# Attention and two gated feed-forward layers in one kernel: the decay rows of k move to ScalarE's queue, and the order of the first loads changes

## The chip, the core and the metric

The kernel runs on one core of a Trainium2 chip. The metric is the time of one execution on the device in microseconds. Three runs of the kernel before took 955.3, 936.14 and 935.29 us; their median is 936.14.

TensorE (PE) multiplies matrices, VectorE (DVE) and ScalarE (ACT) do elementwise work and reductions, GpSimd (POOL) does some of the elementwise work. DMAs are issued from two queues here: SyncE's (SP), which does nothing else, and ScalarE's, where an issue stands between the computing instructions and is reached only when those ahead of it have been handed on.

## The reference

Four batches with eight heads, 576 positions and head size 64 go through attention with a forget gate; the eight heads of a token are then joined to 512 columns, and 2304 tokens go through two feed-forward layers, all of it in float32 by the reference:

```python
scores = scale * np.matmul(q, k.transpose(0, 1, 3, 2))
log_f = np.log(np.clip(f, 0.0001, 1.0))
cum = np.cumsum(log_f, axis=-1)
decay = cum[:, :, :, None] - cum[:, :, None, :]
scores = np.where(causal, -1000000000.0, scores + decay)
attn = softmax(scores)                      # over the last axis
x = np.matmul(attn, v)                      # heads joined: 2304 x 512
h = x @ w_in;  g = h * np.tanh(softplus(h));  x = g @ w_out      # 512 -> 2048 -> 512
out = (sigmoid(x @ w_gate) * (x @ w_val)) @ w_out2               # 512 -> 1536 -> 512
```

The weights arrive as 64-bit floats, read as pairs of 32-bit words.

## The kernel before, in words

**Tiling.** Batch by batch, heads are taken in pairs (four pairs a batch). For each pair the scores of 128 queries against all earlier keys go into PSUM, VectorE adds the causal mask and takes the maximum (`softmax_part`, line 713), ScalarE takes the exponential with the sum (line 764 in the first batch's first part, 862 elsewhere), the weights of attention are transposed and multiplied with v (lines 967 and 979). In the first batch scores are float32 matmuls of 66 rows: 64 of the head, and two that add the decay. One operand, `Q32` (tile `sab`), holds q in rows 0 to 63, the running sum of log f in row 64, and a constant in row 65. The other, `K32` (tile `mab`), holds k in rows 0 to 63, a constant in row 64, and the running sum in row 65. The product of these two rows is the decay.

**The decay rows.** `decay()` loads f, clips it, takes the logarithm, and forms the running sum with one scan on VectorE (line 463) into a float32 tile `cum` (in the trace and the order a piece of `wout`, `wout_90`). Four small DMAs (line 469) copy it into the rows: for q and for k one each for the first 144 positions (`seg` 0) and the next 112 (`seg` 1). The first score of a pair needs only the first piece of k's row, the second (256 columns wide) both. The constants come from memory: line 405 for k's tile, line 407 for q's.

**The other loads at the start.** `prep_first` loads k (line 550) and q (line 552) of a pair, `prep_v` its v (line 623), `constants` an identity matrix (line 397), and `load_w` half a group of weights, 512 KB (line 669). The first four weights, numbers 0 to 3, go out on ScalarE's queue; VectorE turns their 64-bit words into float32 in three passes (lines 641, 645, 649), then ScalarE forms a 16-bit high part (line 506) and VectorE, GpSimd or ScalarE with GpSimd the low part (lines 525, 530 and 534).

**What sets the order.** Every piece of work is a generator that asks for an engine with an estimated duration; `Order` runs a small planner at build time. Each piece has a due time (the second argument of `spawn`, or `od.due`), and of the pieces that could start on an engine the one with the earliest due time goes first. The plan becomes each engine's fixed list of instructions. A load on SP also waits in the plan until the planner's DMA clock is near. The planner decides, too, which engine does a copy or a low part (`scaled`, `rest`), and where it expects TensorE to wait it inserts filler matmuls on the mask (`fill`, line 1085) that compute nothing of use. A change of a due time at the start therefore shifts decisions through the whole program.

**Completion semaphores.** All DMAs, from both queues, take one of eight completion semaphores in turn (DMAHW0 to DMAHW7 in the order). A DMA is issued only once the one that had the same semaphore eight DMAs earlier has landed; that wait stands on the issuing queue and holds everything behind it.

Of the kernel before, what the change touches and what calls it, by code (L numbers as in the profile page):

```python
# [58 lines left out]
class Order:  # L59
# [32 lines left out]
    def spawn(self, gen, due):  # L92
        self.n += 1
        t = {"time": self.now(), "due": due, "n": self.n, "gen": gen, "lag": 0.0}
        self.step(t, None)
# [214 lines left out]
def attention_moe_moe_kernel(ctx, tc, qk, v, f, carry, ident, const, rows_q, rows_k, w_in, w_out, w_gate, w_val, w_out2, out):  # L310
    nc = tc.nc
# [29 lines left out]
    od = Order(BUFS)  # L341
    done, give, pick, spawn = od.done, od.give, od.pick, od.spawn

    def take(*tags, turn=()):
        return (yield ("take", tags, *turn))

    def need(*keys):
        yield ("need", keys)
# [22 lines left out]
    def words(t, o, n):  # L371
        return t.rearrange("p a b c -> p (a b c)")[:, o:o + n]
# [18 lines left out]
    KF = 66  # L391
    K32 = MAB.rearrange("p a q h s -> p a q (h s)").bitcast(FP32)
    Q32 = SAB.rearrange("p a q h s -> p a q (h s)").bitcast(FP32)
# [41 lines left out]
    def decay():  # L435
# [26 lines left out]
        yield "DVE", t_dve(SL)  # L462
        nc.vector.tensor_tensor_scan(out=cum, data0=ft, data1=zt, initial=car, op0=ALU.add, op1=ALU.add)

        for row, key in ((Q32[64:65], "rq"), (K32[65:KF], "rk")):
            for seg in range(2):
                n = min(SL, 256 - seg * SL)
                yield "SP", 0.5, 10000, (key, seg)
                nc.sync.dma_start(
                    out=row.rearrange("o a q s -> o (a q) s")[:, :, seg * SL:seg * SL + n],  # L470
                    in_=cum[seg * NH:seg * NH + 2 * NPB, 0:n],
                )
# [180 lines left out]
    def load_w(hi, lo, src, scale, key, n):  # L653

        if n:
            yield from need(("st", n - 1) if n < NFIRST else ("rk", 1))

        if n in XPLACE:
            yield from take(turn=("wr", n))
            raw = words(XPLACE[n], 0, 2048)  # L660
        else:
            (ri,) = yield from take("wr", turn=("wr", n))
            raw = words(xt[2 + (ri % 3 == 0)], ri % 3 // 2 * 2048, 2048)
        raw = raw.bitcast(I32).rearrange("p (n t) -> p n t", t=2)
        due = od.cur["due"]
        if n < NFIRST:
            od.due((-40, -30.1, -28.8, -27.8)[n])
        yield "SP", 0.5, 128 * 4096
        (nc.scalar if n < NFIRST else nc.sync).dma_start(
            out=raw.rearrange("p n t -> p (n t)").rearrange("p (a n) -> p a n", a=src.shape[1]), in_=src  # L670
        )
        od.due(due)
        (fi,) = yield from take("wf", turn=("wf", n))
        w = words(xt[4], fi % 2 * 1024, 1024).bitcast(I32)
        yield from float32(w, raw)
        if n not in XPLACE:
            give("wr", ri)
        w = w.bitcast(FP32)
        if len(hi.shape) == 3:
            w = w.rearrange("p (a n) -> p a n", a=hi.shape[1])  # L680
        yield from scaled(hi, w, scale, 512)
        yield from rest(lo, w, scale, hi, 512, WP0 <= n < WPOOL)
        give("wf", fi)
        done(key)
# [856 lines left out]
    NFIRST = 4  # L1541
    XPLACE = {2: win[5], 3: win[4]}
    spawn(decay(), -50)
    nl = ns = no = 0
    for b in range(NB):

        if b:
            end = ((b * S + 256) // 256) * 8 - LEAD
            mid = end - SPAN
            beg = mid - SPANA  # L1550
            if b == 1:
                beg, mid = beg + LATE, mid + LATE
            spans = ((beg, mid), (mid, end))
        else:
            end = at_step[1, 0] - LEAD
            mid = end - B0
            beg = -30.0
            spans = ((beg, beg + 4.5), (mid, end), (end + 1, end + 1 + C4))
        pre = PRE if b else 0.0
        for p in range(NPB):  # L1560
            spawn(prep(b, p, 0, ("ld", nl)) if b else prep_first(p, 0, ("ld", nl)), beg + p - pre)
            nl += 1
            if b == 0 and p == 3:
                spawn(constants(), beg)
                spawn(masks(), beg)
                spawn(ones(), beg - 1)
# [97 lines left out]
```

## Time and profile before

| what | value |
|---|---|
| runs | 955.3, 936.14, 935.29 us |
| profiled execution, its own time | 933.85 us |
| its span, first to last instruction | 932.1 us |
| mean granted clock of TensorE | 0.989 |
| busy: PE, DVE, ACT, POOL | 907.0, 591.5, 556.9, 74.9 us |
| DMA traffic | 90.50 MB, mean 97 GB/s |

The profiled execution takes 1.75 us more than its span, and it is 2.3 us under the median of the runs. Busy time is a mean over stages with different limits: TensorE is busy 97% of the span, yet that share holds fillers and the slow first stage. A row of a timeline gives the start in us from the span's start, the duration, engine, line, operation and tiles, the number of instructions merged into it, and in square brackets how long the engine had been idle before and what released it. ACTq and SPq are the queues that issue DMAs: the duration there is that of the issue, not of the transfer. A transfer's landing has no row of its own; it shows as the release of whoever waited for it.

### The profile page before, as it was taken

The numbers are of one execution on the slowest core, as the hardware profiler recorded it, in microseconds if no ns is written. First come the engines' busy times: TensorE is split into PE (matmuls) and PEld (weight loads), VectorE is DVE, ScalarE is ACT, GpSimd is POOL, SyncE is SP. The second block draws the span as 40 slices with busy tenths as digits, with TensorE's granted clock in tenths as the row PEclk, the third lists the DMA queues.
The fourth block names the chain that finished last, engine by engine and source line by source line (L and its number), as shares of the span: only waits on it lengthen the run. The fifth ranks groups of instructions, "written<-read, shape, count | busy, mean of one in ns | idle before, by whom it ended". The sixth has DMA issues, their size and how long they took to land.

```text
span 932.1 us, 20975 instructions
## 1 busy us (share of the span) xinstructions
PE 907.0 (97%) x8599; PEld 715.8 (77%) x8599; DVE 591.5 (63%) x1352; ACT 556.9 (60%) x1093; POOL 74.9 (8%) x75
## 2 busy tenths in 40 slices
PE   7999899999999999999999999999999999999998
PEld 5667678778887888878888887777777777777776
DVE  5889989766667745675799999963236133432333
ACT  4878689788888977978445465544325332432343
POOL 0011211111111101000100010110000000000000
PEclk7989999999999999999999999999999999999999
DMA  6687986568457655644344433200000000100000
GB/s 203 185 189 191 228 241 169 119 122 160 120 124 136 122 135 107 119 91 71 105 136 136 148 129 109 69 12 34 1 1 35 13 1 1 47 1 2 12 36 23
DMA packets 145426, 90.50 MB, mean 97 GB/s; under 512 B 103626, under 2 KB 127138, under 8 KB 145329
## 3 DMA queue, kind: packets, MB, share of 16 engines
q1 hardware_dynamic: 144242, 87.07, 38.3%
q10 hardware_dynamic: 1088, 2.10, 0.7%
q8 instruction: 67, 1.10, 0.5%
q14 instruction: 29, 0.23, 0.1%
HBM read 50.79 MB, written 4.84 MB: 60 GB/s over the span
## 4 chain that ended last, share of the span: by engine, by line
PE 66%; DVE 10%; DMA 4%; ACT 2%; issue 1%; SPq 0%; ACTq 0%; DVEq 0%
PE bank L1358 8%; PE bank L1360 8%; PE bank L1359 8%; PE o_acc L1506 5%; PE o_acc L1505 5%; PE o_acc L1504 5%; PE h_ps L1070 4%; PE y_ps L1120 4%; PE h_ps L1072 4%; PE h_ps L1071 4%; PE y_ps L1122 4%; PE y_ps L1121 4%; PE o_ps L979 3%; DMA wraw<-w_gate 2%; DVE wf L649 2%; DVE wf L645 1%
## 5 line engine op out<-in xcount | busy, mean ns | idle before, releaser
L1120 PE MATMUL y_ps<-g,wout 128*128 128x256 f16 x576 | 157.2, 273 | 2.8 <-ACT wout L506 2.2
L1121 PE MATMUL y_ps<-g,wout 128*128 128x256 f16 x576 | 157.0, 273 | 2.4 <-DVE wout L525 2.4
L1070 PE MATMUL h_ps<-xt,win 128*128 128x256 f16 x576 | 157.3, 273 | 2.0 <-ACT h_ps L1033 1.2
L1071 PE MATMUL h_ps<-xt,win 128*128 128x256 f16 x576 | 156.9, 272 | 0.1
L1122 PE MATMUL y_ps<-g,wout 128*128 128x256 f16 x576 | 157.0, 273 | 0.0
L1072 PE MATMUL h_ps<-xt,win 128*128 128x256 f16 x576 | 156.9, 272 | 0.0
L1448 DVE TENSOR_TENSOR v<-bank,e 128x512 f32<-128x512 f32 (+1 forms) x30 | 19.1, 637 | 165.2 <-ACT bank L1365 164.9
L1365 ACT ACTIVATE bank<-bank 128x512 f32<-128x512 f32 (+1 forms) x90 | 48.5, 539 | 92.8 <-PE bank L1360 90.7
L525 DVE SCALAR_TENSOR_TENSOR pp<-sp,sm,pp 128x512 f16<-128x512 f32 (+4 forms) x126 | 80.5, 653 | 20.1 <-ACT pp L506 19.0
L713 DVE CUSTOM_DVE_ANT_0 sp<-s_ps,mask 128x512 f32<-128x512 f32 (+4 forms) x144 | 67.2, 492 | 17.6 <-PE s_ps L847 14.8
L862 ACT ACTIVATE sp<-sp,sm 128x384 f32<-128x384 f32 (+3 forms) x112 | 63.7, 570 | 15.8 <-DVE sm L713 15.2
L506 ACT ACTIVATE pp<-sp,sm 128x384 f16<-128x384 f32 (+4 forms) x112 | 65.1, 603 | 7.3 <-DVE sm L738 3.5
L1070 PEld LDWEIGHTS <-win 128*128 128x128 f16 x576 | 56.2, 98 | 17.0 <-issue 3.4
L1071 PEld LDWEIGHTS <-win 128*128 128x128 f16 x576 | 56.4, 98 | 11.3 <-issue 2.6
L1120 PEld LDWEIGHTS <-wout 128*128 128x128 f16 x576 | 56.3, 98 | 11.2 <-ACT wout L506 2.7
L1121 PEld LDWEIGHTS <-wout 128*128 128x128 f16 x576 | 56.3, 98 | 10.7 <-DVE wout L525 3.0
L1043 DVE SCALAR_TENSOR_TENSOR g<-h_ps,g 128x512 f16<-128x512 f32 x72 | 49.3, 687 | 23.1 <-ACT g L1039 22.9
L1072 PEld LDWEIGHTS <-win 128*128 128x128 f16 x576 | 56.2, 98 | 7.0 <-issue 0.3
L1122 PEld LDWEIGHTS <-wout 128*128 128x128 f16 x576 | 56.3, 98 | 6.5
L1033 ACT ACTIVATE h_ps<-h_ps 128x512 f32<-128x512 f32 x72 | 41.8, 584 | 14.0 <-PE h_ps L1072 13.7
L979 PEld LDWEIGHTS <-vt 128*64 128x64 f16 x1368 | 36.2, 112 | 14.2 <-issue 12.9
L534 POOL TENSOR_TENSOR low<-st,mab 128x512 f16<-128x512 f32 (+1 forms) x24 | 32.4, 1352 | 160.8 <-ACT mab L506 144.7
(208 smaller groups left out, 2290.4 us busy)
## 6 DMA issues: line engine op xcount, KB each, us to landing
xt<-w_out SPq DMA_DIRECT2D x16, 512.0 KB
xt<-w_in SPq DMA_DIRECT2D x12, 512.0 KB
wraw<-w_gate SPq DMA_DIRECT2D x12, 512.0 KB
wraw<-w_val SPq DMA_DIRECT2D x12, 512.0 KB
wraw<-w_out SPq DMA_DIRECT2D x12, 512.0 KB
out<-ob SPq DMA_DIRECT2D x18, 256.0 KB
vst<-v SPq DMA_DIRECT2D x12, 320.0 KB
st<-qk SPq DMA_DIRECT2D x12, 320.0 KB
```

Source lines behind the costliest of these rows:

```text
L506: nc.scalar.activation(out=dst, in_=src, func=ACTF.Copy, scale=scale, bias=bias)
L525: nc.vector.scalar_tensor_tensor(dst, a, scale, b, op0=ALU.mult, op1=ALU.subtract)
L713: nc.vector.tensor_tensor_reduce(out=sp, in0=ps_ap, in1=mk, op0=ALU.add, op1=ALU.min, scale=-0.125, scalar=1.0e38, accum_out=mn,)
L1070: nc.tensor.matmul(dst, lhsT=wh, rhs=xh, start=(k == 0), stop=False)
L1071: nc.tensor.matmul(dst, lhsT=wh, rhs=xl, start=False, stop=False)
L1072: nc.tensor.matmul(dst, lhsT=wl, rhs=xh, start=False, stop=(k == KD - 1))
L1120: nc.tensor.matmul(dst, lhsT=wh, rhs=gh, start=first, stop=False, skip_group_check=True)
L1121: nc.tensor.matmul(dst, lhsT=wl, rhs=gh, start=False, stop=False, skip_group_check=True)
L1122: nc.tensor.matmul(dst, lhsT=wh, rhs=gl, start=False, stop=last, skip_group_check=True)
L1358: nc.tensor.matmul(dst, lhsT=wh, rhs=xh[:, k], start=first, stop=False, skip_group_check=True)
L1359: nc.tensor.matmul(dst, lhsT=wh, rhs=xl[:, k], start=False, stop=False, skip_group_check=True)
L1360: nc.tensor.matmul(dst, lhsT=wl, rhs=xh[:, k], start=False, stop=last, skip_group_check=True)
```

## The change

Four edits. The rows of k (`rk`) are issued by ScalarE instead of SP, and the two loops are turned round, so that the order is q and k of piece 0, then q and k of piece 1. The third and fourth weights are issued by SP instead of ScalarE, and the first two weights get earlier due times. The second weight is no longer held in the plan until the third and fourth wait for the rows. The first two pairs of q and k get due times ahead of the rows.

```diff
--- before.py
+++ after.py
@@ -462,11 +462,11 @@
         yield "DVE", t_dve(SL)
         nc.vector.tensor_tensor_scan(out=cum, data0=ft, data1=zt, initial=car, op0=ALU.add, op1=ALU.add)
 
-        for row, key in ((Q32[64:65], "rq"), (K32[65:KF], "rk")):
-            for seg in range(2):
+        for seg in range(2):
+            for row, key in ((Q32[64:65], "rq"), (K32[65:KF], "rk")):
                 n = min(SL, 256 - seg * SL)
                 yield "SP", 0.5, 10000, (key, seg)
-                nc.sync.dma_start(
+                (nc.scalar if key == "rk" else nc.sync).dma_start(
                     out=row.rearrange("o a q s -> o (a q) s")[:, :, seg * SL:seg * SL + n],
                     in_=cum[seg * NH:seg * NH + 2 * NPB, 0:n],
                 )
@@ -653,7 +653,7 @@
     def load_w(hi, lo, src, scale, key, n):
 
         if n:
-            yield from need(("st", n - 1) if n < NFIRST else ("rk", 1))
+            yield from need(("st", 0) if n == 1 else ("rk", 1))
 
         if n in XPLACE:
             yield from take(turn=("wr", n))
@@ -664,9 +664,9 @@
         raw = raw.bitcast(I32).rearrange("p (n t) -> p n t", t=2)
         due = od.cur["due"]
         if n < NFIRST:
-            od.due((-40, -30.1, -28.8, -27.8)[n])
+            od.due((-49.95, -49.5, -28.8, -27.8)[n])
         yield "SP", 0.5, 128 * 4096
-        (nc.scalar if n < NFIRST else nc.sync).dma_start(
+        (nc.scalar if n < 2 else nc.sync).dma_start(
             out=raw.rearrange("p n t -> p (n t)").rearrange("p (a n) -> p a n", a=src.shape[1]), in_=src
         )
         od.due(due)
@@ -1558,7 +1558,9 @@
             spans = ((beg, beg + 4.5), (mid, end), (end + 1, end + 1 + C4))
         pre = PRE if b else 0.0
         for p in range(NPB):
-            spawn(prep(b, p, 0, ("ld", nl)) if b else prep_first(p, 0, ("ld", nl)), beg + p - pre)
+
+            ahead = 19.9 + 0.9 * p if b == 0 and p < 2 else 0
+            spawn(prep(b, p, 0, ("ld", nl)) if b else prep_first(p, 0, ("ld", nl)), beg + p - pre - ahead)
             nl += 1
             if b == 0 and p == 3:
                 spawn(constants(), beg)
```

In the program that comes of it the lists of all engines differ. Two places matter at the start, and VectorE's list shows what they do to it.

SP from its fourth row on (after the loads of f and of the matrix that carries the sums), before; `mab` is k's tile, `sab` q's, `wout_90` the running sums, `win_83` the identity, `xt_72` v:

```order
L405 DMA mab<-const 1x4608
L407 DMA sab<-const 1x2560
L550 DMA mab<-qk 64x2x256
L552 DMA sab<-qk 64x2x256
L397 DMA win_83<-ident 128x128 [waits DMAHW1_49]
L469 DMA sab<-wout_90 1x8x144 [waits DMAHW2_49,DVE_49]
L469 DMA sab<-wout_90 1x8x112 [waits DMAHW3_49]
L469 DMA mab<-wout_90 1x8x144 [waits DMAHW4_49]
L469 DMA mab<-wout_90 1x8x112 [waits DMAHW5_49]
L550 DMA mab<-qk 64x2x256 [waits DMAHW6_49]
L552 DMA sab<-qk 64x2x256 [waits DMAHW7_49]
L623 DMA xt_72<-v 128x640 [waits DMAHW0_49]
```

and now:

```order
L550 DMA mab<-qk 64x2x256
L552 DMA sab<-qk 64x2x256
L550 DMA mab<-qk 64x2x256
L552 DMA sab<-qk 64x2x256
L405 DMA mab<-const 1x4608
L469 DMA sab<-wout_90 1x8x144 [waits DMAHW1_49,DVE_49]
L469 DMA sab<-wout_90 1x8x112 [waits DMAHW3_49]
L407 DMA sab<-const 1x2560 [waits DMAHW5_49]
L397 DMA win_83<-ident 128x128 [waits DMAHW6_49]
L550 DMA mab<-qk 64x2x256 [waits DMAHW7_49]
L623 DMA xt_72<-v 128x640 [waits DMAHW0_49]
L669 DMA win_81<-w_in 128x2x512 [waits DMAHW1_49]
```

The second pair's loads (lines 550 and 552) stand ahead of the rows of line 469. The constants for q's tile, line 407, went from the second place shown to behind q's two rows, the identity behind them, and the third and fourth weights (line 669, `win_81` and `win_80`) stand between the loads of v.

ScalarE from its start, before; line 669 are weights, line 452 the logarithm, line 506 the high part of the first weights, line 764 the first exponentials:

```order
L669 DMA xt_74<-w_in 128x2x512
L452 ACT_TABLE_LOAD
L452 ACTIVATE wout_91,wout_84<-wout_91 128x144 [waits DVE_49]
L453 ACT_TABLE_LOAD
L453 ACTIVATE wout_84<-wout_84 128x1
L669 DMA xt_73<-w_in 128x2x512
L506 ACTIVATE win_76<-xt_75 128x512 [waits DVE_49]
L669 DMA win_81<-w_in 128x2x512 [waits DMAHW0_49]
```

and now:

```order
L669 DMA xt_74<-w_in 128x2x512
L452 ACT_TABLE_LOAD
L452 ACTIVATE wout_91,wout_84<-wout_91 128x144 [waits DVE_49]
L453 ACT_TABLE_LOAD
L453 ACTIVATE wout_84<-wout_84 128x1
L669 DMA xt_73<-w_in 128x2x512 [waits DMAHW0_49]
L469 DMA mab<-wout_90 1x8x144 [waits DMAHW2_49,DVE_49]
L506 ACTIVATE win_76<-xt_75 128x512 [waits DVE_49]
L469 DMA mab<-wout_90 1x8x112 [waits DMAHW4_49]
```

The second weight (`xt_73`) now waits for DMAHW0, which the first weight holds. The two rows of k stand around the first weight's high part, and the third weight is gone from between.

VectorE from the end of the first weight's conversion, before; line 713 (printed as ISA) is the reduction of a score, its second row for each score, which only reads out the maximum, is left out here:

```order
L649 SCALAR_TENSOR_TENSOR xt_75<-xt_74,xt_75 128x512 [waits DVE_49]
L525 SCALAR_TENSOR_TENSOR win_76<-xt_75,win_76 128x512 [waits Activation_49]
L641 TENSOR_SCALAR xt_75<-xt_73 128x512 [waits DMAHW5_49]
L645 SCALAR_TENSOR_TENSOR xt_75<-xt_73,xt_75 128x512 [waits DVE_49]
L713 ISA wout_88,sm<-s_ps,mask 128x128 [waits PE_49]
L713 ISA wout_88,sm<-s_ps,mask 128x128
L649 SCALAR_TENSOR_TENSOR xt_75<-xt_73,xt_75 128x512 [waits DVE_49]
L713 ISA wout_88,sm<-s_ps,mask 128x256 [waits PE_49]
```

and now:

```order
L649 SCALAR_TENSOR_TENSOR xt_75<-xt_74,xt_75 128x512 [waits DVE_49]
L525 SCALAR_TENSOR_TENSOR win_76<-xt_75,win_76 128x512 [waits Activation_49]
L641 TENSOR_SCALAR xt_75<-xt_73 128x512 [waits DMAHW0_49]
L645 SCALAR_TENSOR_TENSOR xt_75<-xt_73,xt_75 128x512 [waits DVE_49]
L649 SCALAR_TENSOR_TENSOR xt_75<-xt_73,xt_75 128x512 [waits DVE_49]
L713 ISA wout_88,sm<-s_ps,mask 128x128 [waits PE_49]
L713 ISA wout_88,sm<-s_ps,mask 128x128
L525 SCALAR_TENSOR_TENSOR win_76<-xt_75,win_76 128x512 [waits Activation_49]
L713 ISA wout_88,sm<-s_ps,mask 128x256 [waits PE_49]
```

The second weight is converted whole (lines 641, 645, 649) ahead of the first score's reduction, where its last pass stood behind it; its low part (line 525) stands between the first and the second score's.

Counted over the whole lists, TensorE has the same matmuls but for the fillers, 123 before and 102 now. On VectorE there are six fewer low halves of attention weights (line 525 to `pp`: 28 instead of 32 with 512 columns, 22 instead of 24 with 256), which GpSimd has instead, and three more of `wout` (15 instead of 12). ScalarE has 55 table loads for its functions in the rest of the program instead of 53 (line 862: 19 instead of 20, line 925: 8 instead of 6, line 1033: 28 instead of 27).

## Rows read from the trace of the kernel before

**Rows 1.** Stages: stretch, length, busy PE, PEld, DVE, ACT, POOL; granted clock; DMA.

```profile
10.00:20.00 10.00, 8.10 (x28) 6.57 (x29) 5.86 (x25) 4.99 (x19) 0.00 (x0) 0.50 0.79 227
...
60.00:80.00 20.00, 17.79 (x191) 13.26 (x192) 18.27 (x44) 17.32 (x34) 3.75 (x4) 1.00 0.91 210
80.00:100.00 20.00, 17.88 (x177) 13.51 (x175) 18.42 (x48) 15.25 (x28) 3.73 (x5) 1.00 0.75 186
...
300.00:450.00 150.00, 150.00 (x1748) 124.68 (x1747) 90.06 (x267) 116.80 (x227) 13.63 (x16) 1.00 0.54 104
```

**Rows 2.** The filler's line: ns of one (least, median, most), first and last start.

```profile
L1085 PE MATMUL y_ps<-mask x123: 272/273/421, 1.4 to 101.8; 128*128 128x256 bf16 x123
```

**Rows 3.** Timeline of TensorE: start, us, line, op, tiles, count [idle before, releaser].

```profile
5.52 2.10 PE L1085 MATMUL y_ps<-mask 128*128 128x256 bf16 x14
10.01 1.20 PE L777 MATMUL s_ps<-mab,sab 66*128 66x128 f32 x4 [2.39 <-DMA sab<-wout]
13.09 4.61 PE L777 MATMUL s_ps<-mab,sab 66*128 66x256 f32 x12 [1.89 <-DMA mab<-wout]
```

**Rows 4.** Timeline of SP's queue, the same columns.

```profile
...
2.02 0.22 SPq L407 DMA_DIRECT2D sab<-const  x1
3.64 0.59 SPq L397 DMA_DIRECT2D win<-ident  x1
6.50 1.49 SPq L469 DMA_DIRECT2D sab<-wout  x2
8.04 1.31 SPq L469 DMA_DIRECT2D mab<-wout  x2
9.39 0.60 SPq L550 DMA_DIRECT2D mab<-qk  x1
12.69 0.38 SPq L623 DMA_DIRECT2D xt<-v  x1
...
```

**Rows 5.** Timeline of VectorE.

```profile
...
7.55 0.69 DVE L649 SCALAR_TENSOR_TENSOR xt<-xt,xt 128x512 int32<-128x512 int32 x1
...
9.55 0.42 DVE L641 TENSOR_SCALAR xt<-xt 128x512 int32<-128x512 int32 x1
...
11.24 0.29 DVE L713 CUSTOM_DVE_ANT_0 wout<-s_ps,mask 128x128 f32<-128x128 f32 x1 [0.54 <-PE s_ps L777]
...
15.18 0.42 DVE L713 CUSTOM_DVE_ANT_0 wout<-s_ps,mask 128x256 f32<-128x256 f32 x1 [2.82 <-PE s_ps L777]
...
18.73 0.40 DVE L641 TENSOR_SCALAR xt<-win 128x512 int32<-128x512 int32 x1
...
22.70 0.43 DVE L641 TENSOR_SCALAR xt<-win 128x512 int32<-128x512 int32 x1
```

**Rows 6.** Timeline of ScalarE and its queue.

```profile
...
3.68 0.41 ACTq L669 DMA_DIRECT2D xt<-w_in  x1
...
8.28 0.63 ACT L506 ACTIVATE win<-xt 128x512 f16<-128x512 f32 x1 [2.68 <-DVE xt L649]
8.29 0.38 ACTq L669 DMA_DIRECT2D win<-w_in  x1
...
15.64 0.51 ACT L764 ACTIVATE wout<-wout,sm 128x256 f32<-128x256 f32 x1 [2.62 <-DVE sm L713]
```

**Rows 7.** The table of stages again, from ScalarE's wide exponential to 24 us.

```profile
15.64:24.00 8.36, 8.36 (x35) 6.55 (x35) 6.80 (x29) 6.39 (x25) 0.00 (x0) 0.53 0.75 225
```

**Rows 8.** SP's own waits, 0 to 30 us.

```profile
SPq L550 <- DMA win<-w_in: 3.4, 1, 3.4
SPq L623 <- DMA win<-w_in: 2.0, 1, 2.0
```

**Rows 9.** Groups by line and shape: count, busy us, mean ns, idle before.

```profile
L525 DVE SCALAR_TENSOR_TENSOR pp<-sp,sm,pp 128x512 f16<-128x512 f32 x32 | 24.4, 771 | 2.9 <-ACT pp L506 2.3 <-POOL pp L509 0.6
L525 DVE SCALAR_TENSOR_TENSOR wout<-xt,wout 128x512 f16<-128x512 f32 x12 | 8.9, 742 | 1.6 <-ACT wout L506 1.4
L862 ACT ACT_TABLE_LOAD x20 | 25.7, 1283 | 0.3
```


## The prediction

> **What bounds the kernel now.** I read the table of stages first [rows 1]. The span is 932.1 us and the program around it makes this execution 933.85 us; the three runs have the median 936.14, so a term in the sum moves both alike, and I count from 936.14. In the table the reader is to see two regimes. Late in the program TensorE is busy without a break (150.00 of 150.00 us in 300 to 450). Early on it is not (17.79 and 17.88 of 20 us in 60 to 100). Next I read where its filler matmuls stand [rows 2]: 123 of them, the last at 101.8 us. They compute nothing; the planner puts them where it expects TensorE to wait. So up to about 102 us TensorE waits for others, above all VectorE (18.27 and 18.42 of 20 us in 60 to 100) with ScalarE behind it (17.32 and 15.25) [rows 1]. TensorE's real work is the same list in both kernels: only the filler count differs, 123 before and 102 now. The time can therefore change in two ways: the start-up gets shorter, or the new order leaves other holes later.
>
> Third, the start itself [rows 3, 4]. TensorE stops at 7.62 (5.52 + 2.10), begins the first score at 10.01 after 2.39 us without work, runs its four passes, and waits again 1.89 us until 13.09 for a row of mab: the second piece of k's decay row, whose issue on SP began near 8.70 (the pair of issues runs 1.31 us from 8.04). VectorE sits idle 2.82 us in front of the second score's reduction at 15.18 [rows 5], ScalarE 2.62 us in front of its exponential at 15.64 [rows 6]. That is the hole the change aims at. Fourth, SP's own waits [rows 8]: it stood 2.0 and 3.4 us for two weight loads, because a DMA on SP waits until the DMA that last used its completion semaphore has landed, and those two semaphores were held by the third and fourth weights.
>
> **The change, part by part.**
>
> *The rows.* SP issued the four back to back, 6.50 to 9.35 [rows 4]. Now q's two stay on SP (6.50 and 7.32), k's first goes out on ScalarE at about 6.5 as soon as the scan allows, k's second behind the hi-copy of the first weight, which ran at 8.28 [rows 6]. So k's rows are issued 1.5 and 0.4 us earlier, and no half-megabyte weight goes out in between: the third weight left ScalarE at 8.29, just ahead of k's second row, and that row took 4.4 us from issue (8.70) to use (13.09). The third row, with nothing new beside it, took 1.97 us (8.04 to 10.01).
>
> *What is late next.* The order shows what the diff does not say: the row of constants for q (L407) moves from SP's fourth place, issued at 2.02, to behind q's two rows, and the first score now waits for it. SP is through with q's rows at 7.99, so it is issued at about 8.0. No row shows how long it takes; the nearest are the two above, 1.97 and 4.4 us, so it lands between 10.0 and 12.4. For less than 1.97 nothing speaks, and for more than 4.4 nothing either, as the weight that made the 4.4 is gone from there. I take 10.5, near the short end: 1.97 plus half a microsecond, because the second weight now comes later. It used to be issued at 3.68 [rows 6]; now it waits on ScalarE for the first weight's landing, and two more 128 KB loads stand ahead of the rows, less 64 KB for the identity, 192 KB more in all. At the 227 GB/s of 10 to 20 us [rows 1] that is 0.85 us of queue, part of it inside the 1.97. VectorE has time to convert the second weight meanwhile: it began that at 9.55, and the three passes take 0.42 + 0.69 + 0.69 = 1.8 us [rows 5].
>
> *The first two scores.* From the first score's start to its reduction it is 1.23 us (10.01 to 11.24), from the second's to its own 2.09 (13.09 to 15.18) [rows 3, 5]. k's second row, issued at 8.28, lands by 10.3 at 1.97 us, so the second score follows without a wait: reduction at 10.5 + 1.23 + 2.09 = 13.8 instead of 15.18. **Gain 1.35 us**; between 1.9 (row at 10.0) and a loss of 0.5 (row at 12.4).
>
> *The second pair, and SP's queue.* k and q of pair two went out from 9.39 on and made nobody wait; alone they are worth nothing, but with both pairs there, scores one to four run back to back. Behind them SP sends, by its own issue lengths (0.2, 0.6, 0.6 and 0.4 us) [rows 4], the first v at about 9.5 instead of 12.69, the third weight at 9.9 (before 8.29) and the fourth, three issues later, at 11.5. VectorE took up the third at 18.73 and the fourth at 22.70 [rows 5]; both have time. From 15.64 to 24 ScalarE is busy 6.39 of 8.36 us [rows 7], so it waits 1.97: more than that cannot be regained, since it is then full. In the new order pair three's scores and the fourth weight no longer stand behind late loads, so I take a third, **0.65 us**, with 0 and 1.97 as ends. The work that hides the later third weight is the scores; were it late past 17 us, VectorE would pay each microsecond.
>
> *From there to 102 us* I count the gain one for one: VectorE, with ScalarE, paces this stretch and TensorE waits in it. If a load bound instead, it could go to zero.
>
> *The new order elsewhere.* The planner decides everything afresh. Counted in the two orders, six low halves of P leave VectorE for GpSimd (four of 512 columns at 0.771 us; with the two smaller ones at the same price 4.6 us) and three low halves of w_out come back (3 x 0.742 = 2.2) [rows 9]: 2.4 us at best. Against it stand two more of ScalarE's table loads, 55 instead of 53, at 1.283 us each [rows 9]: 2.6 us at worst. Both engines have some slack in every stage of [rows 1], so neither need reach TensorE; I take 0.
>
> **Sum:** 1.35 + 0.65 = 2.0 us. 933.85 becomes 931.85 for a profiled execution, 936.14 becomes **934.1**.
>
> **The rivals.**
>
> *Only the issue time.* Queue and landing are two things: all rows share the 16 DMA engines with the second weight, which now itself leaves later. If the landing of k's second row follows its issue, 8.70 to 8.28, and nothing else improves, the gain is 0.4 us: **935.7**. For it: DMA is at a share of 0.79 in 10 to 20 us [rows 1]. Against: the weight that overtook this row is gone from its path. The Trainium skill (Trainium Kernel Development and Optimization, Key Constraints) says that issuing from several engines saves only the issuing sequencer's time, since all transfers run on the same 16 engines; it speaks for this rival, and the row's 4.4 us beside a load from another queue agrees with it. Chance 0.2.
>
> *The constant row becomes the wait.* If L407's row needs more than 3.86 us from its issue, it comes after 11.86, and then 11.86 + 3.32 = 15.18: the hole is as long as before. At 4.4 us the reduction is 0.5 us late; with the 0.85 us of queue on top 1.4 us late, and SP's earlier loads meet a full ScalarE. Slower: 936.6 to **937.5**. For it: it is one partition, 10 KB, behind both rows, and nothing else in TensorE's first wait is issued as late. Against: the 1.97 us. Chance 0.2.
>
> *More than the start.* Row at 10.0, all of ScalarE's waits gone, VectorE relieved: 1.9 + 1.97 + 2.4 = 6.3 us, **929.9**. TensorE's granted clock was 0.50, that is 1.2 GHz, in 10 to 20 us, after its wait of 2.39 us and with the one of 1.89 in it [rows 1, 3]; one wait instead of two could bring the full clock sooner, which is part of this case. Chance 0.12.
>
> That the change does not do what it says can be excluded for the issue order; that the whole planned order is worse by the two table loads, 936.14 - 2.0 + 2.6 = 936.7, gets 0.08. My forecast has 0.4.
>
> **How the numbers follow.** The best case, less the 0.9 us by which the two nearer runs differ, gives 929.0, which I round to 929.5; the worst, 0.5 + 2.6 late, 939.2, with the same 0.9 gives 940. About two in ten lie outside, for runs as far off as the 955.3 shown and for an order that falls out differently. Two per cent, what a measurement tells from no change, is 18.7 us: faster needs 917.4, four times the visible waits of the start (2.39 + 1.89), 0.01; slower needs 954.9, 0.02; within 0.97.
>
> **What would show it.** In the changed profile: TensorE's first score at about 10.5, released by the constants' or the last row's DMA, no second wait before the 256-wide score, VectorE's reduction of it near 13.8, ScalarE's first wide exponential near 14.3, no 2 and 3.4 us of SP waiting on weights, the last filler near 100 us. First score after 11.9: the second rival. First score early but 256-wide score still waiting: the first. Start two microseconds earlier and the same end: the gain was lost between 30 and 200 us, and the table of stages must show more TensorE idle there than now. My forecast falls if VectorE's idle time before 31 us is as long as it was.

## The result and the profile after

| | before | changed |
|---|---|---|
| median of 15 runs, us | 934.91 | 944.05 |
| all runs, us | 933.14 to 955.3 | 936.15 to 947.41 |
| profiled execution, its span, us | 933.85, 932.1 | 936.15, 934.3 |

The changed kernel is slower: ratio 1.0082, 95% interval 1.0067 to 1.0097, some 8 us; the medians lie 9.1 us apart. (The run of 955.3 us is not in the ratio.) That is under two per cent, but outside the forecast range, on its slow side. The profiled execution of the changed kernel was the shortest of its 15; a second trace, of a typical one, follows with the experiments.

**The start went as forecast, or better.** TensorE, VectorE and ScalarE of the changed kernel, in the columns of [rows 3]:

```profile
10.62 5.11 PE L777 MATMUL s_ps<-mab,sab 66*128 66x128 f32 x16 [2.99 <-DMA sab<-const]
```

```profile
13.21 0.42 DVE L713 CUSTOM_DVE_ANT_0 wout<-s_ps,mask 128x256 f32<-128x256 f32 x1 [0.30 <-PE s_ps L777]
```

```profile
8.38 0.64 ACTq L469 DMA_DIRECT2D mab<-wout  x1
...
13.68 0.51 ACT L764 ACTIVATE wout<-wout,sm 128x256 f32<-128x256 f32 x1 [0.72 <-DVE sm L713]
```

The first score is released by the row of constants (L407) and 16 passes run in one piece, where 4 and 12 stood with a wait between. The second score's reduction comes 1.97 us sooner than in [rows 5], the wide exponential 1.96 sooner than in [rows 6]. k's second row went out at 8.38, with 8.28 forecast. SP's issues, and what it waited for in the first 30 us:

```profile
8.18 0.40 SPq L407 DMA_DIRECT2D sab<-const  x1
...
10.32 0.43 SPq L669 DMA_DIRECT2D win<-w_in  x1
...
12.06 0.43 SPq L669 DMA_DIRECT2D win<-w_in  x1
```

```profile
SPq L550 <- DMA win<-w_in: 1.9, 1, 1.9
...
SPq L476 <- DMA win<-w_in: 0.7, 1, 0.7
```

The row of constants took 10.62 - 8.18 = 2.44 us from issue to use, between the 1.97 and 4.4 that I had as ends. The third and fourth weights (L669) went out at 10.32 and 12.06, with 9.9 and 11.5 forecast. The stages that answer to [rows 1] and [rows 7]:

```profile
10.00:20.00 10.00, 9.38 (x33) 7.46 (x34) 7.73 (x34) 6.38 (x26) 0.72 (x1) 0.55 0.93 258
...
60.00:80.00 20.00, 17.94 (x172) 13.91 (x169) 19.64 (x44) 16.73 (x33) 4.13 (x4) 1.00 0.69 185
```

```profile
13.68:24.00 10.32, 10.32 (x50) 8.49 (x49) 8.52 (x39) 8.45 (x32) 0.00 (x0) 0.63 0.97 251
```

TensorE is busy 9.38 us in 10 to 20, not 8.10, and in 60 to 80 VectorE paces more than before, with 19.64 of 20 us. The last filler starts at 97.9 us instead of 101.8 [rows 2].

**The loss stands at 165 to 190 us**, between two of the stages of [rows 1]. The table of stages there, before:

```profile
165.00:170.00 5.00, 4.90 (x45) 4.14 (x43) 3.94 (x9) 3.85 (x9) 0.00 (x0) 1.00 0.69 140
170.00:175.00 5.00, 5.00 (x62) 3.83 (x62) 2.67 (x9) 4.30 (x10) 0.00 (x0) 1.00 0.68 134
175.00:180.00 5.00, 3.93 (x46) 2.95 (x41) 4.68 (x11) 2.90 (x6) 0.20 (x1) 1.00 0.40 79
180.00:185.00 5.00, 4.89 (x56) 3.87 (x55) 3.81 (x16) 4.03 (x10) 0.00 (x0) 1.00 0.50 110
```

and of the changed kernel, with the late stage that shows nothing:

```profile
165.00:170.00 5.00, 3.94 (x49) 3.32 (x47) 3.64 (x7) 4.97 (x11) 1.19 (x1) 1.00 0.33 94
170.00:175.00 5.00, 3.59 (x29) 2.69 (x28) 3.89 (x9) 4.09 (x9) 0.87 (x2) 1.00 0.49 105
175.00:180.00 5.00, 2.18 (x28) 1.34 (x28) 3.94 (x15) 4.06 (x9) 0.30 (x1) 0.83 0.92 189
180.00:185.00 5.00, 3.90 (x29) 2.46 (x29) 3.69 (x11) 3.36 (x10) 2.27 (x3) 0.50 0.68 129
300.00:450.00 150.00, 150.00 (x1724) 124.67 (x1722) 91.38 (x267) 118.73 (x229) 14.04 (x16) 1.00 0.54 105
```

TensorE falls from 18.72 busy us of these 20 to 13.61, and its granted clock to 0.50 (1.2 GHz). What it waits for there, in its timeline:

```profile
172.45 0.27 PE L1122 MATMUL y_ps<-g,wout 128*128 128x256 f16 x1
...
175.58 0.44 PE L909 MATMUL s_ps<-mab,sab 128*64 128x288 f16 x4 [1.99 <-DVE sm L713]
176.79 0.44 PE L909 MATMUL s_ps<-mab,sab 128*64 128x288 f16 x4 [0.77 <-DVE sm L713]
177.04 0.70 PE L979 MATMUL o_ps<-pt,vt 128*64 128x128 f16 x18
178.39 0.48 PE L846 MATMUL s_ps<-mab,sab 128*128 128x384 f16 x1 [0.65 <-DVE sm L713]
...
181.10 1.17 PE L979 MATMUL o_ps<-pt,vt 128*64 128x128 f16 x18 [1.92 <-DVE xt L1005]
...
183.67 0.42 PE L1070 MATMUL h_ps<-xt,win 128*128 128x256 f16 x1
```

The row at 172.45 is the last feed-forward matmul of the first two blocks of tokens. The third block's first step needs the second batch's first attention part of all four pairs, and until it goes on at 183.67 TensorE has nothing but scores and products with v, each behind VectorE or ScalarE. ScalarE at that time:

```profile
177.50 1.32 ACT L506 ACTIVATE pp<-sp,sm 128x512 f16<-128x512 f32 x2
178.85 0.72 ACT L530 ACTIVATE sp<-sp,sm 128x512 f32<-128x512 f32 x1
179.47 0.76 ACT L925 ACTIVATE sp<-sp,sm 128x576 f32<-128x576 f32 x1
180.14 0.19 ACT L925 ACTIVATION_READ_ACCUMULATOR sp<-sp,sm 128x1 f32 x1
180.23 0.36 ACT L1002 ACTIVATE xt<-o_ps 128x256 f16<-128x256 f32 x1
```

The product that ended at 177.74 (177.04 + 0.70) waits 2.5 us for its copy out of PSUM (L1002), which stands behind attention weights and an exponential in ScalarE's list; only then do VectorE's L1005 and the product at 181.10 follow.

**A count of progress.** To see where a trace gains or loses I added up TensorE's real work: each matmul that is no filler by its columns (float32 twice, 256 columns as 0.109 us, the distance of two starts at a granted clock of 1.00). The difference between the time and the work done by then is what is lost so far. How many us a profiled run is ahead of the profiled run of before (minus: behind), at six times; the last column agrees with the spans within 0.1 us. The runs beside the changed kernel are explained below:

```
at us               50    100   160   190   300   900
changed             3.9   3.9   5.2  -2.5  -2.2  -2.2
after_again         3.9   2.6   0.1  -8.0  -9.6  -8.7
e1_rk_act           0.0   1.0   0.4   0.1   1.0   1.5
e2_rk_act_w_sp      0.0   1.0   2.1   1.1   2.6   2.6
e3_plan_only        1.0  -1.1  -0.8  -8.5 -10.5 -12.8
no_ahead            0.0   2.0   1.1   0.2   0.1  -0.5
no_ahead_5          2.4   1.0   1.0   0.2   0.8   0.8
e2_ah               2.4   1.9   1.4  -1.9  -6.3  -8.1
before_late25       0.0  -1.3   0.6  -9.9 -15.3 -15.1
late_m1             2.6   2.3  -4.9  -5.6  -4.2  -6.1
late_p075           2.8   1.9   0.8  -3.0 -10.2 -14.6
hole_fill           2.2   1.5   0.6  -6.3  -6.2  -5.8
```

Two cautions. no_ahead and no_ahead_5 are one program, and their traces differ by 2.4 us at 50 and by 1.0 at 100: so small a difference between two rows is no finding by itself. And a row is one execution: that of late_m1 was the longest of its ten (940.06 us, median 936.48), that of e2_ah took 942.19 at a median of 938.88.

### The profile page after: what moved, and what is told of

Read it like the earlier page. It is cut to its first block, busy times and chain, and to the rows that moved or that the text cites. A ratio compares the mean times of both kernels' runs of the same rounds, so it can differ in the third digit from the quotient of the medians.

```text
span 934.3 us, 20919 instructions
## 1 busy us (share of the span) xinstructions
PE 905.8 (97%) x8578; PEld 714.1 (76%) x8578; DVE 591.6 (63%) x1347; ACT 561.5 (60%) x1100; POOL 78.6 (8%) x80
## 4 chain that ended last, share of the span: by engine, by line
PE 61%; DVE 7%; DMA 3%; ACT 2%; issue 1%; SPq 0%; ACTq 0%; DVEq 0%
PE bank L1358 9%; PE bank L1359 9%; PE bank L1360 9%; PE o_acc L1506 5%; PE o_acc L1504 5%; PE o_acc L1505 5%; PE y_ps L1120 3%; PE h_ps L1070 3%; PE y_ps L1121 3%; PE y_ps L1122 3%; PE h_ps L1071 3%; PE h_ps L1072 3%; PE o_ps L979 2%; DMA wraw<-w_gate 1%; DVE wf L649 1%; DVE wf L645 1%
## 5 line engine op out<-in xcount | busy, mean ns | idle before, releaser
L525 DVE SCALAR_TENSOR_TENSOR pp<-sp,sm,pp 128x384 f16<-128x384 f32 (+4 forms) x120 | 75.8, 640 | 21.3 <-ACT pp L506 19.6
L713 DVE CUSTOM_DVE_ANT_0 sp<-s_ps,mask 128x384 f32<-128x384 f32 (+4 forms) x144 | 67.3, 493 | 18.5 <-PE s_ps L847 16.7
L979 PEld LDWEIGHTS <-vt 128*64 128x64 f16 x1368 | 35.8, 111 | 17.1 <-issue 15.0
L979 PE MATMUL o_ps<-pt,vt 128*64 128x128 f16 (+1 forms) x1368 | 43.9, 214 | 3.8 <-DVE xt L1005 1.9
```

The lines of the kernel that those rows point to most:

```text
L525: nc.vector.scalar_tensor_tensor(dst, a, scale, b, op0=ALU.mult, op1=ALU.subtract)
L713: nc.vector.tensor_tensor_reduce(out=sp, in0=ps_ap, in1=mk, op0=ALU.add, op1=ALU.min, scale=-0.125, scalar=1.0e38, accum_out=mn,)
L979: nc.tensor.matmul(o_ps[64 * hh:64 * hh + 64, col:col + n], lhsT=vv[:, jc, vl, 64 * hh:64 * hh + 64], rhs=ptt[:, k, q0:q0 + n], start=(jc ...
```

## The experiments

Theory 1: the queue moves are a gain, but the due times set off a plan that leaves TensorE without feed-forward work before the second batch's attention is done. Theory 2: the queue moves themselves cost the time. Ratios are to the kernel before, run on the same chip at the same time (its medians: 934.9 to 936.5).

**One queue move, plan as before** (e1_rk_act):

```diff
-                nc.sync.dma_start(
+                (nc.scalar if key == "rk" else nc.sync).dma_start(
```

> The kernel before with one edit: k's decay rows go out on ScalarE's queue; the plan and every other list stay as before. Theory 1 (the new order uses up the feed-forward work of the first two token blocks before the second batch's first attention part is done, TensorE then stands at 165 to 190 us and its granted clock falls): this order does not change there, so 932 to 936 us, TensorE busy about 4.9 of 5 us in 175 to 180 at a granted clock near 1.00. Theory 2 (the moved queues themselves cost the time, by issues that ScalarE carries or loads that collide): slower than before, 938 to 944. Both rows of k stand ahead of the first weight's high part here, so the second score's reduction should come up to 1.5 us sooner than 15.18.

Measured: 934.0 us, ratio 0.9993 (0.998 to 1.0006). No change that can be told. Yet the start moved by more than expected: the second score's reduction comes 3.3 us sooner than in [rows 5], and then TensorE waits 3.48 us for q of the second pair, a load that made nobody wait before. By 50 us nothing of the lead is left (table).

```profile
11.86 0.42 DVE L713 CUSTOM_DVE_ANT_0 wout<-s_ps,mask 128x256 f32<-128x256 f32 x1
```

```profile
14.21 2.90 PE L777 MATMUL s_ps<-mab,sab 66*128 66x128 f32 x8 [3.48 <-DMA sab<-qk]
```

**Both queue moves, plan as before** (e2_rk_act_w_sp): in addition

```diff
-        (nc.scalar if n < NFIRST else nc.sync).dma_start(
+        (nc.scalar if n < 2 else nc.sync).dma_start(
```

> The kernel before with both queue moves (k's rows on ScalarE's queue, third and fourth weights on SP's), every due time and so the plan as before. Theory 1: no hole at 165 to 190 us, 931 to 936 us. Theory 2: all of the moved queues is in here, so it is as slow as the changed kernel, 940 to 947 us.

Measured: 933.34 us, ratio 0.9979 (0.996 to 0.9997). Theory 2 falls: with all of the moved queues the kernel gains 2.0 us (0.3 to 3.7 by the interval). The second score's reduction stands at 11.83, as in the run above, and the second pair's scores follow at 11.92 instead of 14.21:

```profile
11.92 1.55 PE L777 MATMUL s_ps<-mab,sab 66*128 66x128 f32 x8 [1.23 <-DVE xt L649]
```

So the two queue moves alone bring the second score forward by more than the whole change does (13.21), whose row of constants stands behind q's rows. By the count this lead is gone at 50 us, too, and the gain of this trace shows at 100 to 160.

**The plan without the queue moves** (e3_plan_only): the changed kernel with these two lines as before.

> The changed kernel's due times and loop order with the queues of before (k's rows on SP, third and fourth weights on ScalarE), so its planned order without its queue moves. Theory 1: the order is what costs, 940 to 947 us with a wide spread, TensorE busy under 4 of 5 us and a clock below 1.00 somewhere in 165 to 190 us. Theory 2: the order costs nothing, 932 to 937 us.

Measured: 945.98 us, ratio 1.0118 (1.0095 to 1.014). The due times carry the loss. The expected hole stands at the end of the stretch, TensorE 2.26 and 3.10 busy us of 5 at 180 to 190, at 0.81 and 0.50; between 160 and 190 us 7.7 us are lost (table).

**Earlier attention** (late_m1):

```diff
-    LATE = 0.5
+    LATE = -1.0
```

> The changed kernel with one constant, LATE, at -1.0 instead of 0.5: the second batch's attention is due 1.5 steps earlier. Counted in the order, 453, 519, 612 and 636 matmuls of the 768 feed-forward ones of the first two token blocks stand ahead of the four products with v of that part, against 564, 672, 726 and 777 in the changed kernel, so 132 are left behind the last of them. Theory 1: the hole at 165 to 190 us goes and what the start gained stays, 929 to 934 us with a narrow spread. Theory 2, or any cost that lies in the queue moves: 938 to 947 as the changed kernel. If earlier attention only moves VectorE's load forward, into 60 to 100 us, the time lies between, 934 to 940.

Measured: 936.48 us, ratio 1.0013 (0.9992 to 1.0034). Most of the loss is gone, but not by the road expected, and the trace is of the longest of the ten runs: the hole at 170 to 185 is closed (5.00 of 5 us in each row), and another opens. The stage, and TensorE's waits in 95 to 150 us:

```profile
100.00:150.00 50.00, 43.80 (x481) 35.90 (x478) 40.26 (x106) 34.66 (x77) 7.55 (x9) 0.93 0.87 201
```

```profile
PE y_ps L1120 <- ACT wout L506: 1.7, 1, 1.7
PE y_ps L1121 <- DVE wout L525: 1.2, 1, 1.2
PE o_ps L979 <- DMA pt<-pp: 1.2, 1, 1.2
PE y_ps L1120 <- ACT xt L1139: 1.2, 1, 1.2
```

Before had 47.04 of 50 there. The waits for weights of w_out (`wout`) are not what is new. In 95 to 150 us before waits 2.4 and 2.2 us for VectorE's and ScalarE's parts of them, more than the 1.2 and 1.7 here (from 100 us on 2.4 in all, against 2.9):

```profile
PE y_ps L1121 <- DVE wout L525: 2.4, 3, 1.0
PE y_ps L1120 <- ACT wout L506: 2.2, 2, 1.1
```

New are the wait for the transposed attention weights (`pt`), a longer one for a copy of ScalarE (L1139), and a clock of 0.52 in 105 to 110 us and 0.80 in 110 to 115, where before has 1.00. Which of these carries how much is not shown.

**A quarter of a step later** (late_p075): `LATE = 0.75`.

> The changed kernel with one constant, LATE, at 0.75 instead of 0.5. Queues, due times of the loads and the start's order stay as changed; counted in the order, 594, 630, 720 and 756 of the 768 feed-forward matmuls of the first two token blocks stand ahead of the four products with v of the second batch's first part, nearly as in the kernel before (600, 630, 744, 756), where the changed kernel has 564, 672, 726 and all 768. Theory 1 (the second batch's attention comes too late for that work, and that alone turns the gain into a loss): 930 to 934 us, narrow, TensorE busy over 4.5 of 5 us and clock near 1.00 in most of 165 to 190. Rival (something else of the new order costs: the two table loads, the low halves on GpSimd, the later loads): 940 to 946 as the changed kernel.

Measured: 947.97 us, ratio 1.0127 (1.0092 to 1.0163). A miss: the count of feed-forward matmuls, equal to that of before, did not make it as fast. A smaller hole remains (2.92 of 5 us in 170 to 175, at 0.81), and most is lost where the count says nothing. Its stage and waits at 200 to 300 us:

```profile
200.00:300.00 100.00, 91.70 (x1083) 76.24 (x1076) 61.20 (x185) 82.03 (x170) 12.06 (x13) 1.00 0.64 131
```

```profile
PE o_ps L979 <- DMA pt<-pp: 3.9, 3, 2.4
PE o_ps L979 <- DVE sm L713: 1.8, 1, 1.8
PE s_ps L909 <- DVE sm L713: 1.5, 1, 1.5
```

Before was busy 99.27 there. By the count 3.8 us are lost between 160 and 190, and 7.2 between 190 and 300. So the exhausted cover is how the changed kernel loses, not the only way in which a fresh plan does.

**All but the last edit** (no_ahead, and the same once more, no_ahead_5): the changed kernel with

```diff
-            ahead = 19.9 + 0.9 * p if b == 0 and p < 2 else 0
-            spawn(prep(b, p, 0, ("ld", nl)) if b else prep_first(p, 0, ("ld", nl)), beg + p - pre - ahead)
+            spawn(prep(b, p, 0, ("ld", nl)) if b else prep_first(p, 0, ("ld", nl)), beg + p - pre)
```

> The changed kernel without its last edit: the second pair's q and k are not requested ahead of the rows; queues, loop order and the weights' due times are as changed. Counted in the order the second batch's products with v stand at 600, 630, 744 and 756 feed-forward matmuls, as in the kernel before. Theory 1: no hole, 931 to 934.5 us. Rival (the weights' due times or the loop order carry the loss): 938 to 946.

> The same no_ahead in five rounds, beside the run above and against the kernel before: queues, loop order and the weights' due times as changed, the second pair as before. Theory 1: 0.3 to 0.4 per cent under before (931 to 934 us), with an interval that excludes no change. If the first measurement was luck: 934 to 936.

Measured: 932.13 us, ratio 0.9967 (0.9948 to 0.9986), and 931.82 us, ratio 0.9962 (0.9948 to 0.9977). It is faster than both kernels, by 0.3 to 0.4 per cent against before. Two rows of no_ahead_5 in the place of the hole:

```profile
175.00:180.00 5.00, 3.83 (x37) 2.92 (x36) 4.92 (x11) 2.74 (x6) 0.20 (x1) 1.00 0.64 121
180.00:185.00 5.00, 5.00 (x56) 3.88 (x54) 3.30 (x15) 4.19 (x9) 0.18 (x1) 1.00 0.42 94
```

**The last edit alone, with the queue moves** (e2_ah): the lines of the last diff the other way, in e2_rk_act_w_sp.

> The kernel before with both queue moves and the second pair's early due time, nothing else (loop order and weights' due times as before). The plan differs from that of before from the start on; counted in the order, 546, 654, 684 and 753 feed-forward matmuls of the first two token blocks stand ahead of the second batch's four products with v. Theory 1 (the second pair's request alone sets off the worse plan): 937 to 945 us, with TensorE waiting more than before somewhere in 100 to 200 us. Rival (the loss needs all edits together): 931 to 935.

Measured: 938.88 us, ratio 1.0042 (1.0024 to 1.006). The early due time of the first two pairs turns the gain (0.9979) into a loss (1.0042), 6 us apart; with the other edits beside it, it costs twice as much. Most of what this trace loses does not lie in the hole: 3.3 us between 160 and 190, 6.2 behind 190 us (table).

**The early load, without its plan** (ahead_same_plan): no_ahead, but the second pair's two loads are emitted with the first pair's; SP's list has them behind the first pair's, all other lists are word for word those of no_ahead.

```diff
+        if part or p != 1:
             nc.sync.dma_start(out=K32[0:64, :, p, c0:c0 + n], in_=qk[p, 64:128, :, c0:c0 + n])
...
+        for x in [p] if part or p > 1 else [0, 1] if p == 0 else []:
+            if part == 0 and x > p:
+                nc.sync.dma_start(out=K32[0:64, :, x, c0:c0 + n], in_=qk[x, 64:128, :, c0:c0 + n])
```

> The kernel without the second pair's early due time (the run called no_ahead), every list of TensorE, VectorE, ScalarE and GpSimd word for word as there; only SP issues the second pair's q and k right behind the first pair's, ahead of the rows, as the changed kernel does. Theory 1 (the early request costs only through the plan that it sets off): as no_ahead, 931 to 934 us. Rival (the early loads themselves collide with what follows: the rows wait for two more 128 KB loads): 937 or more. If the early loads are worth something by themselves: under 931.

Measured: 932.61 us, ratio 0.9969 (0.9957 to 0.9982), as no_ahead. The load ahead of the rows costs nothing and gives nothing in the end. In its trace the first score comes at 11.46 us instead of 8.88 (no_ahead_5), as q's rows go out behind the loads, at 8.07 instead of 6.52; in return both pairs' scores run in one piece. The due time that asks for the load costs some 11 to 12 us (1.0082 and 1.0098 against 0.9967), through the plan.

**The hole, made in the kernel before** (before_late25): nothing of the change, `LATE = 2.5`.

> The kernel before, queues and loads untouched, with LATE at 2.5 instead of 0.5: the second batch's first attention is due two steps later, and the counts are 648, 741, 774 and 777, that is all 768 matmuls and nine of the next block's first step stand ahead of the last two products with v. Theory 1: this makes the hole in a kernel that has none of the change: 940 to 948 us, a spread of several us, TensorE busy under 4 of 5 us and a granted clock below 1.00 somewhere in 165 to 190. Rival (the hole is not what costs): 934 to 937.

Measured: 951.25 us, ratio 1.0157 (1.0127 to 1.0187). Its table of stages:

```profile
180.00:185.00 5.00, 1.99 (x11) 1.05 (x11) 4.96 (x10) 2.45 (x7) 1.78 (x2) 0.84 0.37 83
185.00:190.00 5.00, 3.77 (x28) 1.73 (x26) 3.60 (x16) 3.18 (x8) 0.00 (x0) 0.50 0.99 182
190.00:200.00 10.00, 7.28 (x78) 4.88 (x79) 6.63 (x20) 6.73 (x15) 1.36 (x2) 0.65 0.74 140
```

The same hole, somewhat longer, without any edit at the start: 10.5 us are lost between 160 and 190, and the trace is 9.9 behind at 190, of 15.1 in the end.

**A second trace of the changed kernel** (after_again).

> The changed kernel once more, for a second trace; its profiled execution was the fastest of its 15 (936.15 against a median of 944.05). Theory 1: 940 to 946 us median, the same hole at 165 to 190 us, and what a longer execution has in addition lies in stretches at a granted clock under 1.00, in that hole or behind it. Rival: the additional time lies in other waits, at a clock of 1.00.

Measured: 945.05 us, ratio 1.0098 (1.0061 to 1.0135); the profiled run took 942.64. The stretch 50 to 60 us, of the first trace and then of this one:

```profile
50.00:60.00 10.00, 8.56 (x91) 5.88 (x90) 9.37 (x23) 9.36 (x18) 1.78 (x2) 1.00 0.80 184
```

```profile
50.00:60.00 10.00, 8.04 (x45) 4.71 (x46) 9.37 (x23) 9.29 (x17) 1.85 (x2) 0.67 0.88 187
```

The clock fell here in one execution and not in the other; in the ten us before it was the other way round, 0.83 and 1.00. By the count both had lost 21.7 us by 50 us, but 23.9 and 27.5 by 60. Yet that is not what makes this run longer in the end: of the 6.5 us between the two, 1.3 are there at 100 us, 5.1 at 160, 5.5 at 190. So the expectation missed the place. Both lose much the same in the hole (7.7 and 8.1 us, from the table); between 95 and 160 this run waits 2.6 us for weights of w_out against 1.7 (17.38 busy us in 100 to 120 against 18.31), and it has a clock of 0.91 in 120 to 140 against 1.00. In it, the whole gain of the start is spent by 160 us.

**The clock held in the hole** (hole_fill): the changed kernel with fillers in front of four waits (the calls of `plug` in the scores and in the product with v are left out here).

```diff
+    def plug():
+        for _ in range(hole["n"].pop(0) if hole.get("n") else 0):
+            nc.tensor.matmul(hole["hp"][:, 256:512], lhsT=mask[:, 0:128], rhs=mask[:, 128:384],
+                             start=True, stop=True, skip_group_check=True)
...
+                        if blk == 2 and k == 3:
+                            hole.update(hp=hp, n=[0, 15, 5, 0, 4, 14])
```

The fillers write into the free half of the bank that holds the half-finished sums of the third block's first step, and the kernel's result comes out changed. A first matmul of a group clears the accumulation state of the whole bank, in the partitions that it writes, here all 128 (the Trainium skill, PSUM — Partial Sum Buffer, The four PSUM rules); the changed result agrees with that. Which instructions run, and in what order, does not depend on these values.

> The changed kernel with 38 matmuls of 256 columns that compute nothing (15, 5, 4 and 14) in front of the four places at 173 to 181 us where TensorE waits; every other instruction and its place is as changed. They cover about 4 of the 5.3 us of those waits and shorten none of them. In the changed kernel TensorE then runs at a granted clock of 0.50 in 180 to 185 us (3.90 us busy) and 0.83 in the 5 before. Theory 1: the clock stays at 1.00 there, which gives back about 2 us, and the 5 us of waits stay: 941 to 943.5 us. Rival (the fallen clock is most of the loss): 935 to 939. If the clock has no share: 944 to 946.

Measured: 940.53 us (939.27 to 941.55), ratio 1.0052 (1.0036 to 1.0068). The stages of the hole, 1.00 throughout:

```profile
175.00:180.00 5.00, 5.00 (x44) 4.08 (x43) 3.83 (x9) 4.07 (x9) 0.79 (x2) 1.00 0.50 106
180.00:185.00 5.00, 4.22 (x52) 2.98 (x49) 3.86 (x15) 4.09 (x8) 0.38 (x1) 1.00 0.91 185
```

One product and the first score behind the hole (L979, L846; L992, L856 in hole_fill, whose lines stand lower), after_again first. The hole's first score stood at 177.95 there and at 177.35 in hole_fill:

```profile
186.50 1.17 PE L979 MATMUL o_ps<-pt,vt 128*64 128x128 f16 x18 [1.92 <-DVE xt L1005]
...
191.10 0.38 PE L846 MATMUL s_ps<-mab,sab 128*128 128x512 f16 x1
```

```profile
186.02 0.69 PE L992 MATMUL o_ps<-pt,vt 128*64 128x128 f16 x18 [0.75 <-DVE xt L1018]
...
189.38 0.38 PE L856 MATMUL s_ps<-mab,sab 128*128 128x512 f16 x1 [0.15 <-DVE sm L713]
```

From one to the other it is 13.15 us at the fallen clock and 12.03 with it held: in the hole the clock costs 1.1 us, net of what the fillers hold up, and the waits the rest of the 7.7 to 8.1. The median came 3.5 to 4.5 us under the two of the changed kernel (by the ratios 2.8 to 4.3), just under the range expected, and seven runs spread over 2.3 us, where the changed kernel's fifteen spread over 11 and its later four over 5.8. Where the other 2 to 3 us come from, the two traces do not settle.

## Why the prediction was wrong

- **The first two scores, 1.35 us: right, a little small.** First score at 10.62 (10.5 forecast), reduction at 13.21 (13.8), wide exponential at 13.68 (14.3), released by the constants. From first score to reduction it is 2.59 us and not the 1.23 + 2.09 = 3.32 of the sum, which puts the second score behind the first one's reduction, while the passes run in one piece. The short end of 1.97 us was misread: by [rows 3] the score at 10.01 was released by a row of q (`sab`), issued at 6.50 or 7.32, and k's row from 8.04 had landed before it, so that it is an upper bound for k's row and no time of the others. The rival by which the row of constants would take too long is out.
- **ScalarE's waits, 0.65 us: not seen.** From the wide exponential to 24 us it was busy 8.45 of 10.32 us, 1.87 us idle against 1.97 [rows 7]. Where the rest of the lead of 3.9 us at 50 us came from is not shown; SP's waits on weights fell to 1.9 and 0.7 us [rows 8], not to none.
- **One for one to 102 us: right in size here, but not as a rule.** The two traces of the changed kernel are 3.9 and 2.6 us ahead at 100. But in e1_rk_act and e2_rk_act_w_sp the second score's reduction is 3.3 us sooner than before, and both are level with before at 50 us and 1.0 ahead at 100: in e1_rk_act the wait for the second pair's q took it, "a load bound instead".
- **"The new order elsewhere … I take 0", at worst 2.6 us: this step failed.** I priced the order by the instructions that change engine, two table loads against low halves [rows 9]. Not their time counts but which work is left to cover which wait: 7.7 to 8.1 us are lost between 160 and 190 us (table). The rival for it had the right sign, a bound of 2.6 us that excluded the size, and 0.08; "an order that falls out differently" stood only among the two in ten outside the range. The last filler, at 101.8 us, was in effect taken for the end of TensorE's waits, and the late stages that I read [rows 1] leave out 100 to 300 us. There before was busy 47.04 of 50 us in 100 to 150, and 3.93 of 5 at 175 to 180 showed a place where its cover is already thin.
- **"Alone they are worth nothing": right for the loads of the second pair** (ahead_same_plan against no_ahead), **wrong for their due time**, which, with the queue moves, makes e2_ah slower than before. That they "made nobody wait" held only while the rows were late: 3.48 us in e1_rk_act.
- **"Only the issue time"**: k's rows on ScalarE's queue alone gave 0.9993, with an interval that holds this rival's 0.4 us, but not by its mechanism. k's second row went out 0.9 us sooner (7.81 against 8.72), the third weight now behind it (8.52) and not ahead of it (8.29), and the second score began 3.5 us sooner (9.59 against 13.09). The rule that a second issuing engine saves only issue time (the Trainium skill, Trainium Kernel Development and Optimization, Key Constraints) fits the kernel's time. In the trace it was not issue time that counted: the row, no longer behind a large load, took 1.8 us from issue to use instead of 4.4. Taking the weights off ScalarE's queue, too, brought 2.0 us. That this is the size of my sum is chance: it came without the early loads, and not one for one from the start.
- **The range.** 929.0 made into 929.5 is no rounding; nothing hangs on it, as the time left the range at its other end, 940.
- **"Start two microseconds earlier and the same end: the gain was lost between 30 and 200 us"** is what happened, and more than the gain went.

Shown is that the due time of the first two pairs sets the loss off, that the queue moves do not, and that a hole at this place, made in the kernel before, costs at least as much (10.5 us against 7.7 to 8.1). Not settled is the share of each place in a fresh plan: e2_ah and late_p075 lose more behind 190 us than in the hole.

## What to carry to other kernels

Where one planner orders the whole program, a due time at the start is a new program: change the queue and the place of a load without it (as in e2_rk_act_w_sp and ahead_same_plan), or time the new plan as a kernel of its own. A lead at the start counts only as far as the next wait: in e1_rk_act 3.3 us of it went into the next load. Before a reordering is taken at zero, look in the stages between start and steady state for the place where the cover is thinnest, and ask what the new order leaves there. One trace can be of the shortest of many executions: compare its time with the median before reading a cause from it.

## What the runs showed of the hardware

The granted clock fell to 0.50 (180 to 185 us of the changed kernel) behind a stretch with 2.18 busy us of 5 in which no single wait was longer than 1.99 us. Two executions of the same program had a clock of 1.00 and 0.67 in 50 to 60 us, and 0.83 and 1.00 in the ten us before; their work lay 3.6 us apart by 60 us, and the waits that the profile names in 48 to 62 us were 1.4 and 2.0 us. k's small second row took 4.4 us from issue to use behind a 512 KB load that had gone out 0.43 us before it on the other queue, and 1.8 us (7.81 to 9.59) in e1_rk_act, where that load came behind it. With the clock held in the hole the seven runs spread over 2.3 us.
